# Attention followed by a SoLU feed-forward: the order of POOL's sums and one ACT scaling at the start of the last stage, and the PSUM tiles of the first transpositions

## The chip, the cores and the metric

The kernel runs on one core of a Trainium2 chip. It has five instruction streams that run beside each other and meet at semaphores: PE (matrix multiplication and transposition, results in PSUM), ACT (activation functions and copies), DVE (elementwise work, reductions, 32x32 transposition), POOL (elementwise work on SBUF), and SP, which here issues the DMAs. The metric is the device time of one execution in microseconds, the median of several runs. Inputs and outputs are float32.

## The reference

```python
def rmsnorm(x, g):
    rms = np.sqrt(np.mean(x * x, axis=-1, keepdims=True) + 1e-06)
    return x / rms * g
q_n, k_n = rmsnorm(q, g_q), rmsnorm(k, g_k)              # 8 x 12 heads x 448 x 64
scores = (1 / np.sqrt(64)) * q_n @ k_n.transpose(0, 1, 3, 2)
attn = softmax(scores)
x = (attn @ v)  ->  (8 * 448) x (12 * 64) = 3584 x 768
h = x @ w_in                                             # 3584 x 1024
solu = h * softmax(h)
ln = (solu - mean) / np.sqrt(var + 1e-06) * g_ln
out = ln @ w_out                                         # 3584 x 768
```

## The kernel before

`fast_path` has three stages, one after the other. A slower general path stands behind a test at the end and is not taken with these inputs.

**Attention.** The 96 heads are taken as 48 pairs of heads (n), two pairs to a step (m = 0 to 23). For most pairs the rows of q and k are loaded in a blocked layout, squared on ACT (`squares`), summed on DVE (`row_sums`), folded across partitions on POOL (`fold_sums`), turned into reciprocal roots (`rsqrt_seed` on ACT, `rsqrt_step` on DVE), multiplied on POOL (`normalise`) and transposed in 32x32 blocks on DVE (`qk_transpose`). Each pair then has scores on PE, an exponential on ACT (L809), and the products with v on PE. Sums of exponentials go by DVE (`add`, L846), POOL (`add_more`, L858) and a matmul with ones.

Pairs 0 and 1, the first step, take a shorter way: `load_rows`, `square_rows`, `sum_rows`, `normalise_rows` (L775, DVE), then `transpose_rows` on PE (L783) into a PSUM tile, four transpositions for the queries (s = 0) and four for the keys (s = 1), and `take_rows` copies the result to `qkT`: the queries by ACT (L791), the keys by ACT for pair 0 (L793) and by DVE for pair 1 (L795). The order written out by hand in step 0 is: both halves of pair 0 transposed, both copied; scores 0, 1 and 2 of pair 0; then for pair 1 transposition and copy of the queries, transposition and copy of the keys; squares of pairs 2 and 3; the sums of pair 0's exponentials; and `scores_last` (L832), which makes the last 64 rows of both pairs in one tile and so needs both pairs' `qkT`.

PSUM has eight banks of 512 float32. The pool `ps_t` deals them out as three tiles with the tag "t" and one with the tag "o", of two banks each. The tag "t" serves the scores and small products in turn, each waiting until the tile three before it has been read. The tag "o" holds the products with v (`values_last`, L863) and before them the warm-up products (L764) and the first pairs' transpositions (L780).

**First product, x @ w_in.** 14 groups g of two tiles of 128 tokens (t). The multiplication is done by a scheme with seven products of half size instead of eight. When a tile's row is complete, `done` hands out its remaining steps with due times in units: `ff_max`, `ff_exp` (ACT, L1109), `ff_mult` (DVE, L1113), `ff_moments` (statistics on DVE, L1121 to L1126, then a power and a product on POOL, L1127 and L1129), `ff_norm` (ACT, L1133: the scaling) and `ff_spread` (DVE transposition L1142 and four stores by SP, L1145). The due times of the last four tiles are written out (L1154 to L1156). A unit of this stage counts 4; a step is issued after the first unit that reaches its due time.

**Last product, ln @ w_out.** Seven blocks n of four tiles, with two levels of the seven-product scheme: seven outer products (`ORDER`: P1, P5, P6, P2, P7, P3, P4), each of seven inner products of four 128x192 matmuls (L1253). Each inner product has a slot: outer product q has its seven at 7q + (0, 4, 8, 10, 12, 16, 20). A slot counts 1 in the same clock as above, so the steps still due from the stage before are issued between the first slots; a slot that holds no product only moves the clock. Side work is told to slots by `when`, and is issued after the product of its slot and after the steps that are due:

- `load_u` (SP, L1190) loads a tile's half; `make` builds an outer operand from it: a11, a12, a22 by ACT copies (L1208 to L1212), s1, s3, s4 by DVE, s2 by DVE, or in block 0 by POOL (L1216, slots 0 and 1).
- `inner_sums` makes the four sums or differences that an operand's inner products need, all on POOL (L1231 to L1234). For block 0 the sums of a11 and s1 are made in the stage before, those of s2 (operand of P6, the third outer product) at slot 5, the next ones at slot 7q - 6 (a12 at 15, s3 at 22).
- Results are taken out of PSUM by ACT copies (L1265) for P1 and P5, and by DVE additions (L1267, L1292, L1305, L1315) for the others. The inner products p1, p6, p7 and p4 accumulate in one bank A, so each of them must wait until the one before it has been read.

Each engine works through its instructions in the order in which they were issued, so the place of a call in this program is its place in the queue.

Of the kernel before, what the change touches and what calls it, by code (L numbers as in the profile page):

```python
# [9 lines left out]
FP32 = mybir.dt.float32  # L10
# [356 lines left out]
def fast_path(  # L367
# [25 lines left out]
    B, H, S, D = q.shape  # L393
    DM, DFF = moe_w_in.shape
    P = 128
# [8 lines left out]
    NG = NT // 2  # L404
# [16 lines left out]
    ps_t = banks_in.enter_context(tc.tile_pool(name="ps_t", bufs=3, space=bass.MemoryType.PSUM))  # L421
# [346 lines left out]
    def flat(x):  # L768
        return x.rearrange("p h j d -> p (h j d)")
# [6 lines left out]

    def transpose_rows(n, s):
        d = st[n]
        if s == 0:
            d["pt"] = ps_t.tile([P, 2, 512], FP32, tag="o", name="pt", bufs=1)  # L780
        d["pt", s] = d["pt"][:, s, 0:S]
        for j in range(4):
            nc.tensor.transpose(  # L783
                d["pt", s].rearrange("p (r j) -> p j r", j=4)[:, j], flat(d["sq"][:, s])[:, j * P : (j + 1) * P], ident[0:R, 0:R]
            )
# [189 lines left out]
    def load_x(g):  # L975
        x = gs[g, "x"] = xs.tile([P, KD, 2 * P], FP32, tag="x", name="xg")
        t = 2 * g * P
        while t < 2 * (g + 1) * P:
            b, c = divmod(t, S)
            n = min(S - c, 2 * (g + 1) * P - t)  # L980
            o = t - 2 * g * P

            (nc.sync if g < 2 else nc.scalar).dma_start(x[:, :, o : o + n], xd[b].rearrange("(c p) t -> p c t", p=P)[:, :, c : c + n])
            t += n

    def sizes(g):

        x = gs[g, "x"].rearrange("p c t -> p (c t)")
        n = HD * 2 * P
        sm = gs[g, "s"] = xs.tile([P, 3, HD, P], FP32, tag="x", name="xsum")  # L990
        y = sm.rearrange("p k c t -> p (k c t)")
        if g == 0:
            y = work.tile([P, 2 * NB, 32], FP32, tag="sq", name="sq", bufs=2).rearrange("p b d -> p (b d)")
        for i in range(2):
            nc.scalar.activation(
                y[:, 0:n], x[:, i * n : (i + 1) * n], AF.Square,
                accum_out=xmax[:, 2 * g + i : 2 * g + i + 1],
            )
# [7 lines left out]
    def block_sums(g, part):  # L1006

        if part == 0:
            gs[g, "A"] = x_blocks(g)
        a11, a12, a21, a22 = gs[g, "A"]  # L1010
        sm = gs[g, "s"]
        s1, s2, s4 = [sm[:, i] for i in range(3)]
        if part == 0:
            nc.gpsimd.tensor_tensor(s1, a21, a22, OP.add)
            nc.gpsimd.tensor_tensor(s2, s1, a11, OP.subtract)
        else:
            nc.gpsimd.tensor_tensor(a21, a11, a21, OP.subtract)
            nc.gpsimd.tensor_tensor(s4, a12, s2, OP.subtract)
# [81 lines left out]
    def ff_max(t):  # L1100
        d = mt[t]
        d["nmax"] = small.tile([P, 1], FP32, tag="hmax", name="hmax")
        nc.vector.tensor_scalar(d["nmax"], d["top"], -1.0, None, OP.mult)  # L1103
# [46 lines left out]
    def in_parts():  # L1150
        def done(g, i):
            t = 2 * g + i
            ff_max(t)
            waits = {  # L1154
                (NG - 2, 1): (1, 2, 3, 5, 5), (NG - 2, 0): (1, 2, 4, 6, 7),
                (NG - 1, 1): (1, 2, 3.25, 6.75, 7.25), (NG - 1, 0): (2.25, 4.25, 6.75, 8, 8.75),  # L1156
            }.get((g, i), (1, 2, 3, 5, 7))
            for x, f in zip(waits, (ff_exp, ff_mult, ff_moments, ff_norm, ff_spread)):
                later(x, lambda f=f: f(t))

        p = [products(g, lambda i, g=g: done(g, i)) for g in range(NG)]
        parts = [p[0][1], p[0][2]]
        for g in range(NG):
            turn = [p[g][6], p[g][5], p[g][7], p[g][4], p[g][3]]
            x = len(parts)
            if g + 1 < NG:
                turn[3:] = [p[g + 1][1], p[g][4], p[g + 1][2], p[g][3]]
            parts += turn
            if g + 1 < NG:
                follow(parts, x, lambda g=g: sizes(g + 1))  # L1170
                follow(parts, x + 1, lambda g=g: block_sums(g + 1, 0))
                follow(parts, x + 2, lambda g=g: block_sums(g + 1, 1))
            if g + 2 < NG:
                follow(parts, x + 4, lambda g=g: load_x(g + 2))
        return parts

    ORDER = ("P1", "P5", "P6", "P2", "P7", "P3", "P4")
    STEP = 7
# [8 lines left out]
    def load_u(n, t, h):  # L1187
        own = last.get("u", last["first"])
        r = us[n, "raw", t, h] = own.tile([P, P * HF], FP32, tag="raw", name="ur", bufs=2 if own is last["first"] else 6)
        nc.sync.dma_start(r, ud[4 * n + t][h].rearrange("g j x -> (g j) x"))  # L1190
# [31 lines left out]
    def inner_sums(n, name):  # L1222

        own = last.get("u", last["first"])
        a = us[n, name]
        sm = us[n, name, "sums"] = own.tile(
            [P, 4, KC, 4, 32], FP32, tag="sums", name="sums", bufs=2 if own is last["first"] else 4
        )
        a11, a12, a21, a22 = [a[:, t, k * KC : (k + 1) * KC] for t in range(2) for k in range(2)]
        s1, s2, s3, s4 = [sm[:, i] for i in range(4)]  # L1230
        nc.gpsimd.tensor_tensor(s1, a21, a22, OP.add)  # L1231
        nc.gpsimd.tensor_tensor(s2, s1, a11, OP.subtract)
        nc.gpsimd.tensor_tensor(s3, a11, a21, OP.subtract)  # L1233
        nc.gpsimd.tensor_tensor(s4, a12, s2, OP.subtract)  # L1234
# [104 lines left out]
    def both(n, x, t):  # L1339

        if (n, x) not in us:
            us[n, x] = out_tile(x)
        nc.vector.tensor_tensor(us[n, x][:, t], us[n, "U2" if x == "V" else "U3"][:, t], us[n, "P5"][:, t], OP.add)
        if x == "C22" and t == 0:
            store_y(n, us[n, x], 1, 1)

    def follow(p, i, f):
        g = p[i]

        def both():  # L1350
            g()
            later(1, f)

        p[i] = both
# [7 lines left out]
    def later(units, f):  # L1362
        todo.append((now + 4 * units, f))
# [49 lines left out]
    with tc.manual_schedule():  # L1413
# [10 lines left out]
        for s in range(2):  # L1424
            normalise_rows(0, s)
            transpose_rows(0, s)
# [6 lines left out]
        for m in range(NQ):  # L1433
# [21 lines left out]
            if m == 0:  # L1455
# [6 lines left out]
                for s in range(2):  # L1462
                    transpose_rows(1, s)
                    take_rows(1, s)
# [155 lines left out]
        def when(slot, f):  # L1620
            at.setdefault(slot, []).append(f)

        def made(n, name, *slots_of):
            for t, slot in enumerate(slots_of):
                when(slot, lambda t=t: make(n, name, t))

        period = STEP * len(ORDER)
        for n in range(NS):
            base = period * n
            for i, name in enumerate(ORDER):  # L1630
                q = len(ORDER) * n + i
                for place, f in zip(PLACES, outer_product(n, name, q)):
                    assert STEP * q + place not in slots
                    slots[STEP * q + place] = f
                x = HALVES[name][0]
                if q > 1:
                    when(STEP * q - 6 if q > 2 else 5, lambda n=n, x=x: inner_sums(n, x))
            for x, t, slot in (("V", 1, 31), ("V", 0, 34), ("C22", 1, 45), ("C22", 0, 52)):
                when(base + slot, lambda n=n, x=x, t=t: both(n, x, t))
            if n == 0:  # L1640
                continue
            base -= period
            at_load = (10, 11, 15, 16, 17, 18, 21, 22) if n == 1 else (4, 5, 8, 9, 10, 11, 16, 17)
            blocks = (0, 0), (1, 0), (2, 0), (3, 0), (2, 1), (3, 1), (0, 1), (1, 1)
            for slot, (t, h) in zip(at_load, blocks):
                when(base + slot, lambda n=n, t=t, h=h: load_u(n, t, h))
            late = n == 1
            made(n, "a11", base + 12 + 6 * late, base + 15 + 6 * late)
            made(n, "s1", base + 21 + 18 * late, base + 24 + 17 * late)
            made(n, "s2", base + 28 + 15 * late, base + 38 + 7 * late)  # L1650
            made(n, "a12", base + 33, base + 36)
            made(n, "s3", base + 40 + 7 * late, base + 42 + 7 * late)
            made(n, "s4", base + 47 + 4 * late, base + 49 + 4 * late)
            made(n, "a22", base + 53 + 2 * late, base + 55 + 2 * late)
# [99 lines left out]
```

## Time and profile before

| | us |
|---|---|
| timed runs: median (lowest to highest) | 801.15 (801.07 to 801.8) |
| the profiled execution: its own time | 802.04 |
| its span, first to last instruction | 800.2 |

| stretch of the span, us | length | PE busy | DVE busy | ACT busy | POOL busy | DMA share |
|---|---|---|---|---|---|---|
| 0 to 27: first step | 27.0 | 22.76 | 17.09 | 15.80 | 9.42 | 0.89 |
| 27 to 313: attention | 286.0 | 285.30 | 243.89 | 223.13 | 207.83 | 0.79 |
| 313 to 566.5: first product | 253.5 | 253.19 | 179.22 | 135.26 | 142.35 | 0.47 |
| 566.5 to 583: start of the last stage | 16.5 | 14.59 | 15.78 | 10.16 | 10.95 | 0.77 |
| 583 to the end | 217.2 | 210.61 | 153.25 | 88.94 | 153.76 | 0.49 |

How to read the lines of the profile: a line of the timeline gives the start in us from the span's beginning, the duration, the engine, the line of the kernel, the operation, output<-input by the program's names, shapes, and how many instructions were merged; in brackets how long the engine had stood idle before and which engine's work is taken to have ended the wait. PE is the matrix multiplication, PEld its weight load, which overlaps. In the list of waits the numbers are the total, the count and the longest. Who ended a wait is inferred from semaphore events.

### The profile page before, as it was taken

How to read it: one execution, taken by the hardware profiler on the slowest of the kernel's cores; microseconds unless marked ns; L12 is line 12 of the kernel's file. 1: busy time of each engine (PE TensorE's matmuls, PEld its weight loads, DVE VectorE, ACT ScalarE, POOL GpSimd, SP SyncE). 2: the span in 40 equal slices, each digit the busy share in tenths (PEclk: the TensorE clock that was granted, in tenths of full speed). 3: DMA queues.
4: the chain of work that ended last, by engine and by line, in shares of the span. 5: the costliest groups of instructions: out<-in, count | busy, mean ns of one | idle time of the engine just before them, and what ended most of it. 6: DMA issues, size and time to landing. Idle time of an engine off the chain costs nothing.

```text
span 800.2 us, 15287 instructions
## 1 busy us (share of the span) xinstructions
PE 786.5 (98%) x5382; PEld 469.2 (59%) x5382; DVE 609.2 (76%) x1153; ACT 473.3 (59%) x783; POOL 524.3 (66%) x665
## 2 busy tenths in 40 slices
PE   8999999999999999999999999999999999999997
PEld 3344444444444444444444444444789999999996
DVE  6777989889888895487777667776896776866945
ACT  6777888878778773566766544454515455464410
POOL 2666677768877785243466466668597777877861
PEclk9999999999999999999999999999999999999999
DMA  8878798998888742455555445542757557466212
GB/s 165 162 163 166 171 187 195 197 188 170 166 162 176 147 117 71 138 132 151 151 132 143 108 106 145 140 122 52 208 149 234 166 174 255 133 212 236 100 60 84
DMA packets 266913, 122.74 MB, mean 153 GB/s; under 512 B 184012, under 2 KB 251980, under 8 KB 266828
## 3 DMA queue, kind: packets, MB, share of 16 engines
q1 hardware_dynamic: 252988, 111.78, 55.9%
q10 hardware_dynamic: 13840, 9.90, 4.5%
q8 instruction: 44, 0.72, 0.4%
q14 instruction: 41, 0.34, 0.1%
HBM read 84.94 MB, written 36.70 MB: 152 GB/s over the span
## 4 chain that ended last, share of the span: by engine, by line
PE 88%; DVE 4%; POOL 2%; SPq 1%; ACT 1%; DMA 1%; issue 1%; DVEq 0%; ACTq 0%; POOLq 0%
PE A L1253 14%; PE s L819 13%; PE o L883 12%; PE BD L1038 12%; PE A L1038 12%; PE B L1253 7%; PE sm L932 5%; PE C L1038 5%; PE C L1253 3%; PE s L832 2%; PE o L869 2%; SPq L636 1%; PE o L910 1%; DMA ur<-ud 0%; DVE ub L1142 0%
## 5 line engine op out<-in xcount | busy, mean ns | idle before, releaser
L809 ACT ACTIVATE E<-s 128x896 f32<-128x896 f32 x168 | 141.4, 933 | 12.8 <-PE s L819 11.6
L819 PE MATMUL s<-qkT 64*64 64x448 f32 x1152 | 124.0, 544 | 1.6 <-ACT qkT L793 1.2
L883 PE MATMUL o<-E,v 64*64 64x448 f32 x1056 | 107.2, 536 | 0.0
L1127 POOL TENSOR_TENSOR he<-he,mhalf 128x1 f32<-128x1 f32 x28 | 27.3, 975 | 104.2 <-DVE he L1126 99.1
L819 PEld LDWEIGHTS s<-qkT 64*64 64x64 f32 x1152 | 49.8, 163 | 58.2 <-issue 25.2
L858 POOL TENSOR_TENSOR es<-es,E 128x896 f32<-128x896 f32 x23 | 49.1, 2135 | 51.4 <-DVE es L846 51.4
L1253 PE MATMUL A<-w_out,sums 128*128 128x192 f32 x392 | 80.1, 327 | 2.2 <-POOL sums L1233 1.3
L1253 PE MATMUL B<-w_out,sums 128*128 128x192 f32 x392 | 79.9, 326 | 0.4 <-DVE P L1315 0.4
L713 POOL TENSOR_TENSOR qkn<-qk,ny 128x896 f32<-128x896 f32 x46 | 77.1, 1697 | 3.5 <-DVE ny L707 1.5
L1038 PE MATMUL A<-w_in,xg 128*128 128x512 f32 x168 | 74.6, 593 | 0.0
L883 PEld LDWEIGHTS o<-E,v 64*64 64x64 f32 x1056 | 40.6, 133 | 58.0 <-issue 58.0
L1109 ACT ACTIVATE u<-h,hmax 128x1024 f32<-128x1024 f32 x28 | 32.2, 1151 | 66.8 <-DVE hmax L1103 66.8
L1038 PE MATMUL BD<-w_in,xsum 128*128 128x512 f32 x156 | 71.2, 592 | 0.0
L1253 PEld LDWEIGHTS A<-w_out,sums 128*128 128x128 f32 x392 | 66.1, 190 | 3.3 <-POOL sums L1233 1.6
L1253 PEld LDWEIGHTS B<-w_out,sums 128*128 128x128 f32 x392 | 66.3, 190 | 0.8 <-DVE P L1315 0.7
L846 DVE TENSOR_TENSOR es<-E 128x896 f32<-128x896 f32 x48 | 56.9, 1189 | 0.7 <-ACT E L809 0.7
L1038 PEld LDWEIGHTS A<-w_in,xg 128*128 128x128 f32 x168 | 31.8, 190 | 40.1 <-issue 39.3
L723 DVE STREAM_TRANSPOSE qkT<-qkn 128x896 f32<-128x896 f32 x46 | 50.9, 1106 | 4.1 <-POOL qkn L713 4.1
L1038 PEld LDWEIGHTS BD<-w_in,xsum 128*128 128x128 f32 x156 | 29.5, 190 | 37.5 <-issue 35.2
L690 POOL COPY ss<-part 32x56 f32<-32x56 f32 x92 | 47.1, 512 | 6.1 <-DVE part L680 1.9
L680 DVE TENSOR_REDUCE part<-sq 128x28 f32<-128x896 f32 x46 | 47.8, 1077 | 2.2 <-ACT sq L672 2.2
L1253 PE MATMUL A<-w_out,s 128*128 128x192 f32 x224 | 45.7, 326 | 0.0
(160 smaller groups left out, 1665.5 us busy)
## 6 DMA issues: line engine op xcount, KB each, us to landing
ur<-ud SPq DMA_DIRECT2D x60, 256.0 KB, 4.4
ud<-ub SPq DMA_DIRECT2D x112, 128.0 KB, 2.3
xd<-xo SPq DMA_DIRECT2D x48, 224.0 KB, 3.0
qk<-in_q_dram SPq DMA_DIRECT2D x92, 112.0 KB, 3.2
qk<-in_k_dram SPq DMA_DIRECT2D x92, 112.0 KB, 3.1
v<-in_v_dram SPq DMA_DIRECT2D x24, 384.0 KB, 5.2
out_dram<-P SPq DMA_DIRECT2D x19, 384.0 KB, 3.4
raw<-in_moe_w_in_dram SPq DMA_DIRECT2D x12, 512.0 KB, 5.1
```

Of the source, the lines that this page charges most:

```text
L680: nc.vector.tensor_reduce(norms[m]["part"][:, i], st[n]["sq"], AX, OP.add)
L690: e.tensor_copy(ss[g * 32 : g * 32 + 32], part[o * 32 : o * 32 + 32])
L713: e.tensor_tensor(d["qkn"].rearrange("p (s b) d -> p s b d", s=2), d["qk"].rearrange("p s (b d) -> p s b d", d=32), y.rearrange("p (s b) - ...
L723: nc.vector.transpose(d["qkT"].rearrange("p s t -> p (s t)"), d["qkn"].rearrange("p b d -> p (b d)"))
L809: nc.scalar.activation(d["E", kc], s[:, :, 0:S], AF.Exp)
L819: nc.tensor.matmul(s[c : c + D, h, 0:S], d["qkT"][hh, 1, keys], d["qkT"][hh, 0, :], start=True, stop=True,)
L846: nc.vector.tensor_tensor(d["es"], d["E", 0], d["E", 1], OP.add)
L858: e.tensor_tensor(d["es"], d["es"], d["E", 2], OP.add)
L883: x = nc.tensor.matmul(d["o"][h * D : (h + 1) * D, :], quads[m]["v"][pp, i + 2 * h, kc], d["E", kc][pp, h], start=False, stop=(part == 1 a ...
L932: nc.tensor.matmul(sm[g : g + 32, :], ones[:, w], e[:, h, t * S // 2 : (t + 1) * S // 2], start=(x == 0), stop=(x == len(terms) - 1),)
L1038: nc.tensor.matmul(k[bank], a[:, c], w_in[i][:, c], start=begin and c == 0, stop=c == HD - 1, skip_group_check=not begin,)
L1253: nc.tensor.matmul(k[bank], a[:, c].rearrange("p a i -> p (a i)"), w_out[:, area, i, c], start=begin and c == 0, stop=c == KC - 1, skip_gr ...
```

## The change

Three edits. In `transpose_rows` every group of four transpositions gets a PSUM tile of its own and uses the first of its two banks: the tag is "o" for pair 1's queries, and "t" for pair 0's queries and keys and for pair 1's keys. In the due times of tile 0 of group NG - 2 (the last but one group) the scaling `ff_norm` is due at 6.25 units instead of 6, one slot later: it is issued after the first product of the last stage and no longer ahead of it. The sums of s2 for block 0 are told to slot 2 instead of slot 5; POOL's part of `ff_moments` of the tile that is due between them (group NG - 1, tile 1, due at 3.25 units, issued after slot 4) comes behind them and no longer ahead.

```diff
     def transpose_rows(n, s):
         d = st[n]
-        if s == 0:
-            d["pt"] = ps_t.tile([P, 2, 512], FP32, tag="o", name="pt", bufs=1)
-        d["pt", s] = d["pt"][:, s, 0:S]
+        pt = ps_t.tile([P, 2, 512], FP32, tag="o" if n and s == 0 else "t", name="pt", bufs=1 if n and s == 0 else 3)
+        d["pt", s] = pt[:, 0, 0:S]
         for j in range(4):
             nc.tensor.transpose(
...
-                (NG - 2, 1): (1, 2, 3, 5, 5), (NG - 2, 0): (1, 2, 4, 6, 7),
+                (NG - 2, 1): (1, 2, 3, 5, 5), (NG - 2, 0): (1, 2, 4, 6.25, 7),
                 (NG - 1, 1): (1, 2, 3.25, 6.75, 7.25), (NG - 1, 0): (2.25, 4.25, 6.75, 8, 8.75),
...
                 if q > 1:
-                    when(STEP * q - 6 if q > 2 else 5, lambda n=n, x=x: inner_sums(n, x))
+                    when(STEP * q - 6 if q > 2 else 2, lambda n=n, x=x: inner_sums(n, x))
```

## The prediction

> **What bounds the kernel now.** I read the totals first, then what TensorE itself waited for, then the order of instructions at the two places that the diff touches.
>
> ```profile
> span 800.2 us, 15287 instructions
> PE 786.5 (98%) x5382; PEld 469.2 (59%) x5382; DVE 609.2 (76%) x1153; ACT 473.3 (59%) x783; POOL 524.3 (66%) x665
> ```
>
> TensorE is busy for 98% of the span, and the chain that ends last lies on it for 88%. No edit here changes a matmul, so only TensorE's idle time can be won: 800.2 - 786.5 = 13.7 us. The stretches say where it is: 27.0 - 22.8 = 4.2 us before 27 us, 16.5 - 14.6 = 1.9 us between 566.5 and 583 us, 6.6 us after that. The list of what PE waited for has most of it at the edited lines:
>
> ```profile
> PE A L1253 <- POOL sums L1233: 1.3, 1, 1.3
> PE s L819 <- ACT qkT L793: 1.2, 1, 1.2
> PE pt L783 <- ACT qkT L791: 1.1, 1, 1.1
> PE s L832 <- ACT E L809: 0.7, 1, 0.7
> PE A L1253 <- DVE u L1267: 0.6, 2, 0.4
> PE A L1253 <- ACT q L1265: 0.6, 1, 0.6
> ```
>
> The start, in order of time:
>
> ```profile
> 8.38 1.18 PE L783 MATMUL pt<-ident,xsq 112*128 112x112 f32 x8 [0.15 <-DVE xsq L775]
> 9.66 0.64 ACT L791 ACTIVATE qkT<-pt,gcol 128x448 f32<-128x448 f32 x1 [0.17 <-PE pt L783]
> ...
> 14.26 0.65 ACT L791 ACTIVATE qkT<-pt,gcol 128x448 f32<-128x448 f32 x1
> 14.96 0.60 PE L783 MATMUL pt<-ident,xsq 112*128 112x112 f32 x4 [1.14 <-ACT qkT L791]
> 15.67 0.62 DVE L795 COPY qkT<-pt 128x448 f32<-128x448 f32 x1 [2.00 <-PE pt L783]
> 17.37 2.54 ACT L809 ACTIVATE E<-s 128x896 f32<-128x896 f32 x3 [1.16 <-PE s L832]
> ```
>
> PE writes the key half of pair 1's tile only at 14.96, 0.05 us after ACT has read the query half (14.26 + 0.65 = 14.91), though these are different halves: the one tile ties them. At 9.66 ACT reads pair 0's query half only after both halves are written (9.56).
>
> The last stage's first products:
>
> ```profile
> 567.64 1.23 ACT L1133 ACTIVATE u<-u,shift,he 128x1024 f32<-128x1024 f32 x1
> 568.77 0.30 ACT L1265 COPY q<-A 128x192 f32<-128x192 f32 x1
> 569.22 0.89 PE L1253 MATMUL A<-w_out,sums 128*128 128x192 f32 x4 [0.57 <-ACT q L1265]
> 575.09 1.49 DVE L1113 TENSOR_TENSOR u<-h,u 128x1024 f32<-128x1024 f32 x1
> 575.58 1.59 POOL L1232 TENSOR_TENSOR sums<-sums,s 128x256 f32<-128x256 f32 x1
> 577.28 0.62 ACT L1208 COPY a<-ur 128x512 f32<-128x512 f32 x1 [1.19 <-DMA ur<-ud]
> 578.17 0.92 PE L1253 MATMUL A<-w_out,s 128*128 128x192 f32 x4
> 579.85 1.18 DVE L1220 TENSOR_TENSOR s<-a,s 128x512 f32<-128x512 f32 x1
> 580.44 1.17 POOL L1233 TENSOR_TENSOR sums<-a 128x256 f32<-128x256 f32 x1
> 581.22 0.34 DVE L1267 TENSOR_TENSOR u<-A,P 128x192 f32<-128x192 f32 x1
> 581.71 0.89 PE L1253 MATMUL A<-w_out,sums 128*128 128x192 f32 x4 [1.31 <-POOL sums L1233]
> ```
>
> Groups of four matmuls start 0.65 us apart when nothing is late. The start at 569.22 is 0.73 late, 577.22 0.13, 578.17 0.30, 581.71 1.48; with what follows each, 2.9 us. The label at 581.71 names POOL, but that product (slot 26, P6's p7) reads sums finished at 578.31, and it adds to bank A, which DVE's `u<-A,P` of slot 22 must have read: that ends at 581.56. DVE is late there, having been busy almost without a break since 567.77.
>
> **The tiles of the first pairs.** Nothing is added or removed on any engine and no DMA moves; waits go. (a) Pair 0: ACT is done with its squares at 8.34 + 1.15 = 9.49 and the query half's transpositions at about 8.97, so the copy starts at 9.45 instead of 9.66. Both copies, the first scores (10.77) and all that follows come 0.2 earlier. (b) Pair 1: the key half follows the query half directly. Four transpositions take 0.60, so the second four run from 13.6 to 14.1 instead of 14.96 to 15.56, and DVE's copy starts at 14.2 instead of 15.67 (it started 0.11 behind its PE end) and ends at 14.85. ACT's copy of the query half ends at 14.7. The second half of the last-rows scores needs both copies: 14.9 instead of 16.36, so 1.45 earlier. The exponential of these (17.37) then may start at 15.9; ACT before it has squares until 15.62 + 0.60 - 0.2 = 16.0. DVE's first sum of exponentials (16.21) and the row sums move with DVE's copy; their inputs on ACT are squares ending at 15.5 and 16.0, in time for 15.7 and 16.7. POOL's sum (17.44), its fold (19.61), the reciprocal roots (21.82), the normalising (23.27) and the scores at 26.98 hang on these one behind the other. So 1.45 us arrives at 27 us.
>
> What could take it back: the new buffers. Pair 1's key half gets the buffer of the first scores, whose exponential ends at 12.77, 0.8 us before; the last-rows scores get that of the second scores, free at 13.6 for a start at 14.1. The price is whatever that margin is exceeded by. If DVE's copy still went behind ACT's (both write one `qkT`), it would start at 14.77: 0.9 instead of 1.45. Loads don't move: pair 4's squares (23.15, then 21.7) need k loads issued until 18.03, which land 3.1 us later, at 21.1; with the worst landing of the start, 4.2, at 22.2, taking 0.5. From 27 us to 313 PE is busy 285.3 of 286.0 us, so a shift passes through undiminished. Term: -1.45, between -0.9 and -1.6.
>
> **The scaling one slot later** (6 to 6.25). ACT runs `q<-A` (0.30) ahead of the scaling (1.23), not behind. PE's A is ready at 567.35, so the copy ends at 567.95 and the start at 569.22 can be 568.49. The scaling ends 0.2 to 0.3 later, near 569.1; DVE's transposition of that tile starts at 570.27 only, behind its multiply, so neither it nor SP's four stores move, and the next exponential (568.97) follows as before. The 0.7 us doesn't last: the next accumulation into A needs ACT's `u` copy (570.32 to 570.64), which leaves 0.48, and at 578.17 PE needs an `u` copy that ACT holds behind `a<-ur`, whose load was issued at 574.29, behind DVE's `s3` (573.35). Nothing there moves. Term 0, at best -0.1.
>
> **The sums ahead of the moments** (slot 5 to 2). POOL's four sums of s2 took 574.77 to 578.99. Now they follow its two subtractions, which end at 569.00. Alone a sum takes 0.73 and the next starts 0.70 later. DVE's multiply L1113 (567.77, 2.31 long, 1.22 elsewhere) is held up by the second subtraction until 569.0; then DVE or POOL goes on. The nearest row is the one at 575.09: DVE waited there for POOL's sum to end at 575.50, went next, and POOL's following sum became 1.59 long, 0.86 more than alone. So DVE goes first, and the sums run from 570.0 to 572.9, beside DVE's `P<-C,q`, transposition and statistics, which take 0.34, 1.25 and 1.28 beside POOL's sums elsewhere as they do alone. If POOL went first, DVE would be one sum late: +0.73, and with it `s3`, the load, ACT's copy and PE.
> The moments' power on POOL waits for DVE until 573.44 anyway, 0.5 us after the sums end; beyond that margin every us late goes through the scaling at 574.85 to ACT's copies and PE.
> Next on POOL are the a12 sums (578.95 to 582.3 before). Their input is ready at 571.7, so they take the s2 sums' old place, 574.77 to 579.0, with the same collisions. Then POOL is idle at 579.85, where DVE's L1220 was 1.18 beside POOL's 1.17. Alone the same line takes 0.68 (600.55) and the next starts 0.61 later, against 1.10: DVE's `u<-A,P` ends 0.49 earlier, and PE starts at 581.2 instead of 581.71. PE by itself would be ready at 580.2, so the sums at 577.22 and slot 26 no longer bind, DVE does. Everything behind hangs on PE and DVE; the later stops at 599.28 and 603.69 come from a DVE queue that starts at 591.08 on a PE result, so they shift along. Term: -0.5; from +0.2 (0.73 lost, 0.5 won) to -0.9 (PE never later than its own 580.2 plus latency).
>
> The Trainium skill bears on this in "SBUF — State Buffer", section "Who interferes with whom". It says that issue order decides who blocks, and that a VectorE instruction with two SBUF inputs and a GpSimd one that reads SBUF exclude each other for a whole instruction. It speaks against putting POOL work beside L1113: read at its strictest the last stage would lose 0.2 rather than win 0.5. The row at 575.09 has DVE going next, so I keep the row.
>
> **Sum.** -1.45 - 0 - 0.5 = about -1.95. The profiled execution took 802.04 us (span 800.2 and 1.8 around it), 0.9 above the median of the timed runs, 801.15. The terms are differences in the span, so I take them from both: 800.1 for such an execution, 799.2 for the median.
>
> **Rivals.**
> - One term is small. The head gives only 0.9 because the copies stay in order: 801.15 - 0.9 - 0.5 = 799.75. For it: they write one tile; against: the halves of `xsq` are written by DVE (4.12, 0.69) and ACT (4.49) at the same time. 12 in 100.
> - The last stage gives nothing or loses 0.2: 799.7 to 799.9. For it: POOL's first moved sum meets L1113; against: the row at 575.09. 13 in 100.
> - The head's gain is covered: the loads set the start. DMA engines are busy 89% before 27 us. Only the last stage's 0.5 is left: 800.65. Against: the usual landing is 0.6 us ahead of need. 8 in 100.
> - Slower: in the last stage each of the four moved sums gets in ahead of a DVE instruction of the queue that sets 578.17 and 581.71. DVE is 4 x 0.73 = 2.9 late, the a12 sums are pushed back too so the 0.5 isn't won: 801.15 - 1.45 + 2.9 = 802.6. It decides from 1.45 us of lateness on. Against: from 570 to 573 us no large DVE instruction reads two operands from SBUF, and such ones show no lengthening beside POOL. 5 in 100.
> - The forecast, 799.2, its own range 798.6 to 799.6: 62 in 100.
>
> **How the numbers follow.** Range: the forecast's low end, 798.5 (-1.6, -0.9 and a little), up to the covered head, 800.8; outside are the slower case and some unforeseen, under 2 in 10. About 0.2% (1.6 us) is what a measurement here tells from no change, so 799.55 parts faster from same. Faster: nearly all of the forecast's 62 and a few of the near ones, 0.64. Slower by 0.2% needs more than the slower rival's 802.6: 0.05. Same: 0.31.
>
> **What would show it.** Right: no wait of PE at L783 on ACT; the last-rows scores' second half near 14.9; scores of pair 2 at about 25.5 instead of 26.98; `q<-A` before the scaling; POOL's s2 sums ending near 573; L1220's second instruction near 0.68; slot 26 about 0.5 sooner after 566.5 than now (15.2 us). Wrong: PE at 26.98 unmoved (loads), L1113 over 2.31 (POOL first), the power on POOL behind the sums, or PE stops in slots that had none.

## The result, and the profile after

| | before, us | after, us |
|---|---|---|
| timed runs side by side: median (lowest to highest) | 801.77 (801.07 to 802.30), 12 runs | 799.78 (799.10 to 801.65), 12 runs |
| ratio after / before, 95% interval | | 0.9978 (0.9970 to 0.9985) |
| the profiled execution: its own time, span | 802.04, 800.2 | 799.27, 797.5 |

The kernel became 1.99 us faster by the medians. The two profiled spans differ by 2.7 us. Single executions of one kernel scatter by 1 us and more, so the traces tell where time went, and the medians how much. The runs of before fall into two groups, near 801.2 and near 802.1, so its median depends on how many of each a comparison caught (801.31 to 801.81 in those below). In the changed kernel every line from L782 on has a number one lower than before (L783 is L782, L1253 is L1252).

The totals of the page of after:

```profile
span 797.5 us, 15285 instructions
PE 786.1 (99%) x5382; PEld 468.7 (59%) x5382; DVE 608.1 (76%) x1153; ACT 472.2 (59%) x783; POOL 524.3 (66%) x665
```

Busy times are as before (PE 786.5, POOL 524.3): work has not become less, TensorE's idle time has, from 13.7 to 11.4 us. What PE waited for (total, count, longest, in us):

```profile
PE A L1252 <- DVE u L1266: 1.4, 3, 0.8
PE pt L766 <- DVE warm L763: 1.4, 1, 1.4
PE s L818 <- ACT qkT L792: 0.8, 1, 0.8
PE s L831 <- ACT E L808: 0.7, 1, 0.7
PE B L1252 <- DVE P L1314: 0.4, 1, 0.4
PE s L818 <- ACT qkT L727: 0.4, 1, 0.4
PE BD L1037 <- DVE top L1053: 0.2, 1, 0.2
PE pt L782 <- DVE xsq L775: 0.2, 1, 0.2
```

Three lines of before have gone: the transpositions' wait for ACT (1.1), the wait put down to POOL's sums (1.3) and the one for `q` (0.6). The wait for the first `qkT` is 0.8 instead of 1.2, and DVE's `u` is named where POOL was.

The start of after, in order of time:

```profile
8.26 1.27 PE L782 MATMUL pt<-ident,xsq 112*128 112x112 f32 x8 [0.18 <-DVE xsq L775]
9.24 0.61 ACT L790 ACTIVATE qkT<-pt,gcol 128x448 f32<-128x448 f32 x1
...
12.77 0.99 PE L782 MATMUL pt<-ident,xsq 112*128 112x112 f32 x8
...
13.80 0.62 DVE L794 COPY qkT<-pt 128x448 f32<-128x448 f32 x1 [0.58 <-PE pt L782]
13.81 0.65 ACT L790 ACTIVATE qkT<-pt,gcol 128x448 f32<-128x448 f32 x1
...
15.64 2.55 ACT L808 ACTIVATE E<-s 128x896 f32<-128x896 f32 x3
...
25.24 2.22 PE L818 MATMUL s<-qkT 64*64 64x448 f32 x20 [0.39 <-ACT qkT L727]
```

The eight transpositions of pair 1 now run in one go of 0.99 us, where before two groups of four began 1.7 us apart. ACT and DVE read their halves at the same time (13.81, 13.80). The scores of pair 2 begin at 25.24 instead of 26.98. Counted from the first transposition (8.38 before, 8.26 after, a difference that belongs to the start of the execution) it is 18.60 against 16.98: 1.62 us. From there nothing changes until the last stage: between the first score of pair 2 and the first product of the last stage lie 539.5 to 539.6 us in before, in after and in every kernel below.

The first products of the last stage, the first of them in before and then the rows of after:

```profile
566.54 0.81 PE L1253 MATMUL A<-w_out,a 128*128 128x192 f32 x4
...
564.77 0.81 PE L1252 MATMUL A<-w_out,a 128*128 128x192 f32 x4
...
565.73 0.30 ACT L1264 COPY q<-A 128x192 f32<-128x192 f32 x1
565.86 2.31 DVE L1112 TENSOR_TENSOR u<-h,u 128x1024 f32<-128x1024 f32 x1
565.93 1.24 ACT L1132 ACTIVATE u<-u,shift,he 128x1024 f32<-128x1024 f32 x1
...
567.17 1.59 POOL L1230 TENSOR_TENSOR sums<-s 128x256 f32<-128x256 f32 x1
...
575.22 0.62 ACT L1207 COPY a<-ur 128x512 f32<-128x512 f32 x1 [1.04 <-DMA ur<-ud]
...
576.11 0.92 PE L1252 MATMUL A<-w_out,s 128*128 128x192 f32 x4
...
577.78 0.65 DVE L1219 TENSOR_TENSOR s<-a,s 128x512 f32<-128x512 f32 x1
...
578.62 0.35 DVE L1266 TENSOR_TENSOR u<-A,P 128x192 f32<-128x192 f32 x1
...
579.12 0.89 PE L1252 MATMUL A<-w_out,sums 128*128 128x192 f32 x4 [0.78 <-DVE u L1266]
```

`q<-A` is ahead of the scaling. POOL's first moved sum met DVE's multiply: DVE's took 2.31 as before, POOL's 1.59. The second L1219 takes 0.65 instead of 1.18. Slot 26 begins at 579.12, 14.35 us after the stage's first product (564.77); before it was 581.71 - 566.54 = 15.17 us.

In what follows "slot 26" stands for that distance, and "head" for the distance from the first transposition to the scores of pair 2. Before's head of 18.60 is a steady number: the other profiles with the old tiles and the old order have 18.54 to 18.58.

### The profile page after: what moved, and what is told of

Its sections match the earlier page's. It is cut to its first block, busy times and chain, and to the rows that moved or that the text cites. A ratio compares the mean times of both kernels' runs of the same rounds, so it can differ in the third digit from the quotient of the medians.

```text
span 797.5 us, 15285 instructions
## 1 busy us (share of the span) xinstructions
PE 786.1 (99%) x5382; PEld 468.7 (59%) x5382; DVE 608.1 (76%) x1153; ACT 472.2 (59%) x783; POOL 524.3 (66%) x665
## 4 chain that ended last, share of the span: by engine, by line
PE 87%; DVE 5%; SPq 2%; ACT 2%; DMA 2%; issue 1%; POOL 0%; DVEq 0%; ACTq 0%; POOLq 0%
PE A L1252 14%; PE s L818 13%; PE o L882 12%; PE BD L1037 11%; PE A L1037 11%; PE B L1252 7%; PE sm L931 5%; PE C L1037 5%; PE C L1252 3%; PE s L831 2%; PE o L868 2%; SPq L636 1%; DVE ub L1141 1%; PE o L909 1%; DMA ur<-ud 1%
## 5 line engine op out<-in xcount | busy, mean ns | idle before, releaser
L1252 PE MATMUL A<-w_out,sums 128*128 128x192 f32 x392 | 80.0, 327 | 1.3 <-DVE u L1266 1.2
L1252 PE MATMUL B<-w_out,sums 128*128 128x192 f32 x392 | 79.9, 326 | 0.4 <-DVE P L1314 0.4
L1252 PEld LDWEIGHTS A<-w_out,sums 128*128 128x128 f32 x392 | 66.2, 190 | 2.4 <-issue 1.5
L1252 PEld LDWEIGHTS B<-w_out,sums 128*128 128x128 f32 x392 | 66.3, 190 | 0.8 <-DVE P L1314 0.7
L1252 PE MATMUL A<-w_out,s 128*128 128x192 f32 x224 | 45.7, 326 | 0.1
```

What stands on the lines that cost most here:

```text
L1252: nc.tensor.matmul(k[bank], a[:, c].rearrange("p a i -> p (a i)"), w_out[:, area, i, c], start=begin and c == 0, stop=c == KC - 1, skip_gr ...
```

## The experiments

**The tiles alone.**

```diff
-        if s == 0:
-            d["pt"] = ps_t.tile([P, 2, 512], FP32, tag="o", name="pt", bufs=1)
-        d["pt", s] = d["pt"][:, s, 0:S]
+        pt = ps_t.tile([P, 2, 512], FP32, tag="o" if n and s == 0 else "t", name="pt", bufs=1 if n and s == 0 else 3)
+        d["pt", s] = pt[:, 0, 0:S]
```

> The kernel before with the tiles of the first transpositions alone; the last stage as before. My theory: the shared tile makes PE wait for ACT's copy and ACT for the second half, so PE no longer waits at the transpositions, pair 2's first scores start near 25.2 us instead of 26.98, and about 1.6 us arrives at the end: time 0.9980 of before. The stretch from the last stage's first product to slot 26 (P6's p7) stays at 15.0 to 15.2 us. Rival (loads set the start): pair 2's scores stay near 26.9 and the time is that of before. Rival (the head's gain is used up in the attention stage): scores at 25.2, but the last stage's first product still at 566.5.

Measured: 799.50 us against 801.31, ratio 0.9971 (0.9960 to 0.9982); head 16.81, slot 26 15.02. So this edit alone gives, within the intervals, what the whole change gives.

**The scaling alone.**

```diff
-                (NG - 2, 1): (1, 2, 3, 5, 5), (NG - 2, 0): (1, 2, 4, 6, 7),
+                (NG - 2, 1): (1, 2, 3, 5, 5), (NG - 2, 0): (1, 2, 4, 6.25, 7),
```

> The kernel before with the one scaling a slot later alone. My theory: the stop of 0.73 us at slot 8 goes, but PE still stops at slots 23 and 26, which hang on a load behind ACT and on DVE, so from the last stage's first product to slot 26 it is 15.0 to 15.2 us as before; the time is within 0.1% of before. Rival (the gain at slot 8 lasts): slot 26 at 14.5 and the time 0.5 to 0.7 us lower.

Measured: 801.59 against 801.31, ratio 0.9997 (0.9988 to 1.0006). PE's stop of 0.73 us in slot 8 is gone, and slot 26 is at 15.17, exactly where it was: the time comes back as longer stops in slots 12, 22 and 23.

**The sums alone.**

```diff
-                    when(STEP * q - 6 if q > 2 else 5, lambda n=n, x=x: inner_sums(n, x))
+                    when(STEP * q - 6 if q > 2 else 2, lambda n=n, x=x: inner_sums(n, x))
```

> The kernel before with POOL's s2 sums at slot 2 alone. My theory: the stop at slot 8 stays (0.7), POOL's a12 sums take the old place of the s2 sums, DVE's second L1220 falls from 1.18 to 0.66 and slot 26 comes 0.5 us sooner after the last stage's first product, 14.6 instead of 15.17; time 0.9994 of before. Rival (the sums need the scaling's move to win anything): slot 26 stays at 15.0 to 15.2. Rival (POOL's moved sums hold up DVE): L1113 over 2.31 us, slot 26 later than 15.2.

Measured: 801.67 against 801.31, ratio 1.0003 (0.9994 to 1.0012); slot 26 at 15.06, a gain of 0.11 us where about 0.5 was expected. By that number alone this is the rival that the sums need the scaling's move to win anything. Its timeline shows another cause:

```profile
577.71 0.62 ACT L1208 COPY a<-ur 128x512 f32<-128x512 f32 x1 [1.61 <-DMA ur<-ud]
...
578.58 0.36 DVE L1305 TENSOR_TENSOR P<-B,u 128x192 f32<-128x192 f32 x1 [0.58 <-ACT u L1265]
...
580.27 0.65 DVE L1220 TENSOR_TENSOR s<-a,s 128x512 f32<-128x512 f32 x1
```

The forecast 0.65 is there. But ACT's copy `a<-ur` waited 1.61 us for its load (1.19 before), ACT's `u` copy stands behind it, and so DVE stood still for 0.58 us (0.17 before) ahead of `P<-B,u`. From the load's issue to the copy it was 3.62 us here, 2.99 in before.

**The order alone.** The kernel before, with one line added in step 0: both groups of pair 1's transpositions are called before the two copies, still into one tile.

```diff
                 for s in range(2):
                     transpose_rows(1, s)
+                for s in range(2):
                     take_rows(1, s)
```

> The kernel before, one shared tile, with the order alone changed: both halves of pair 1 are transposed before either is copied. It tells what the sharing costs beyond the order. If only PE's write waits for ACT's read, the key half's transpositions run at 13.6 and DVE copies at 14.2, as with separate tiles, and pair 2's scores start near 25.4. If the two reads of a shared tile are kept in order as well, DVE's copy starts only when ACT's has ended, near 14.95, the last rows' second half near 15.7, and pair 2's scores start near 26.1, so half of the gain is the order's and half the tile's.

Measured: one run of 800.98; head 17.77, scores of pair 2 at 26.32. The timeline of it at pair 1:

```profile
13.31 0.99 PE L783 MATMUL pt<-ident,xsq 112*128 112x112 f32 x8
...
14.36 0.65 ACT L791 ACTIVATE qkT<-pt,gcol 128x448 f32<-128x448 f32 x1
...
15.03 0.62 DVE L795 COPY qkT<-pt 128x448 f32<-128x448 f32 x1 [1.27 <-ACT qkT L791]
15.71 0.59 PE L832 MATMUL s<-qkT 64*64 64x448 f32 x2 [0.52 <-DVE qkT L795]
```

The transpositions run in one go here too, but DVE's copy waits for ACT's to end (14.36 + 0.65 = 15.01): with one tile, its two readers on different engines go one after the other. The head is 0.83 us shorter than before's: about the 0.9 instead of 1.45 which the prediction kept as a bound. In the changed kernel both still write one `qkT` and go together, so the shared PSUM tile tied them, not `qkT`.

**Pair 1's keys alone in a tile of their own.** Pair 0 keeps one tile.

```diff
+        pt = ps_t.tile([P, 2, 512], FP32, tag="t", name="pt", bufs=3) if n and s else d["pt"]
-        d["pt", s] = d["pt"][:, s, 0:S]
+        d["pt", s] = pt[:, s, 0:S]
```

> The kernel before with one edit: only the keys of pair 1 get a PSUM tile of their own; pair 0 keeps one tile for both halves. My working puts 0.2 us on pair 0's copy and the rest on pair 1: pair 0's ACT copy stays at about 9.66, the eight transpositions of pair 1 run in one go of about 0.99 from about 13.2, and the scores of pair 2 start at 25.3 to 25.5 (before 26.98, with the whole change 25.24). Rival (pair 0's part gives nothing, ACT's copy only moves a wait): 25.1 to 25.25, as with the whole change. Rival (the gain is made by order and jitter): 26.3, as where only the order was changed.

Measured: one run of 800.18; head 17.31. Its lines are one higher than before's:

```profile
9.49 0.63 ACT L792 ACTIVATE qkT<-pt,gcol 128x448 f32<-128x448 f32 x1 [0.72 <-PE pt L784]
...
13.05 0.98 PE L784 MATMUL pt<-ident,xsq 112*128 112x112 f32 x8
...
14.07 0.62 DVE L796 COPY qkT<-pt 128x448 f32<-128x448 f32 x1 [0.58 <-PE pt L784]
14.09 0.65 ACT L792 ACTIVATE qkT<-pt,gcol 128x448 f32<-128x448 f32 x1
```

So pair 1 gives 18.60 - 17.31 = 1.29. Scores at 25.53 are 0.03 above the range that was expected, and 0.19 counted from the same start (the first transposition is at 8.22 here, 8.38 before).

One profile against one would leave pair 0's part of 1.62 - 1.29 = 0.33 uncertain, but the head can be split at the first scores in every profile. From these to the scores of pair 2 it is 16.20 to 16.21 us with the old tiles and order, 14.93 here, and 14.92 to 14.96 in seven of the eight profiles with the whole edit: pair 1's part is 1.25 to 1.29. In the eighth, the second profile of the changed kernel, it is 15.21: ACT's squares (L672, at 21.52) had waited there for a load.

From the first transposition to the first scores it is 2.32 to 2.39 us with one tile for pair 0 and 1.89 to 2.32 with two. Pair 0's part is therefore 0 to 0.5, and in five of the eight 0.4 to 0.5.

**The sums of a12 late.** The kernel before, with the next four sums on POOL pushed out of the way of DVE.

```diff
-                    when(STEP * q - 6 if q > 2 else 5, lambda n=n, x=x: inner_sums(n, x))
+                    when(STEP * q - 6 if q > 3 else (5, 22)[q - 2], lambda n=n, x=x: inner_sums(n, x))
```

> The kernel before with one edit: the four a12 sums on POOL are told to slot 22 instead of 15, so that they stand behind the last tile's power and product on POOL and not beside DVE's L1113 (the fourth), L1220 and the copies. My theory (slot 26 waits for DVE's u<-A,P, and DVE is slowed by POOL's sums beside it, the wait's label POOL is not the cause): DVE's second L1220 is about 0.65 alone instead of 1.18, its first 0.68, the last multiply 1.23, and slot 26 starts 14.2 to 14.7 us after the first product instead of 15.17; the sums then come too late for a later product, which is 2 us or more late. Rival (slot 26 does read a POOL sum, as the label of the wait said): slot 26 waits for the moved sums, about 20 us after the first product.

Measured: one run of 804.0.

```profile
579.51 0.64 DVE L1220 TENSOR_TENSOR s<-a,s 128x512 f32<-128x512 f32 x1
...
580.35 0.34 DVE L1267 TENSOR_TENSOR u<-A,P 128x192 f32<-128x192 f32 x1
...
580.83 0.89 PE L1253 MATMUL A<-w_out,sums 128*128 128x192 f32 x4 [0.78 <-DVE u L1267]
...
585.18 0.92 PE L1253 MATMUL A<-w_out,sums 128*128 128x192 f32 x4 [2.16 <-POOL sums L1232]
```

Slot 26 begins 14.38 us after the first product though the sums named in before's wait run only after 583 us: the label POOL at 581.71 in before was not the cause, DVE's `u<-A,P` was. How much of the 0.8 us is owed to the moved sums this run doesn't tell: the load came earlier in it (2.67 us from issue to copy), and DVE had no pause ahead of `P<-B,u`. The 0.8 us are lost again at the product that does need the sums, 2.3 us late.

**The load taken out of ACT's way.** The changed kernel, with ACT's two a11 copies of block 1 made at slots 25 and 27.

```diff
-            made(n, "a11", base + 12 + 6 * late, base + 15 + 6 * late)
+            made(n, "a11", base + 12 + 13 * late, base + 15 + 12 * late)
```

> The changed kernel with one edit more: ACT's two a11 copies of block 1 (they wait for a load that landed 2.9 to 3.6 us after its issue) are made at slots 25 and 27 instead of 18 and 21, behind ACT's u and P copies. Theory A (DVE's own queue, busy without a break, sets slot 26, and the load only slot 23): slot 23 (0.29 late after the change) isn't late any more, DVE's addition P<-B,u follows without its 0.09 pause, slot 26 starts 14.1 to 14.3 us after the first product instead of 14.34, the time is 799.4 to 799.8 beside 799.78. Theory B (the load's landing sets slot 26 through ACT's copy): slot 26 comes 0.5 or more sooner, at 13.8 or less, and the time is about 799.2.

Measured: 799.41 against 801.81, ratio 0.9971 (0.9961 to 0.9982). Slot 23 has no stop, slot 26 is at 14.23: theory A by the trace.

**That, and the transposition of the last group's tile 1 later** (due at 7.75 units instead of 7.25).

> The kernel with the later a11 copies of block 1 and, beside that, the transposition and stores of tile 1 of the last group due at 7.75 units instead of 7.25, behind DVE's q<-A,P and u<-A,P. If DVE's queue sets slot 26 (theory A): slot 26 is not or hardly late, at 12.7 to 13.3 us after the first product instead of 14.34; part of it is lost again a few slots later, since the queue on DVE holds the same work; the time falls by 0.2 to 0.8 us, to about 799.2. If the load sets it (theory B): slot 26 at 13.8 or later, time as with the later copies alone.

Measured: 799.61 against 801.81, ratio 0.9975 (0.9965 to 0.9985). Slot 26 is at 13.53, later than expected, because DVE's L1219 moved forward into POOL's sums and took 1.10 again. The next stop takes back more than was won:

```profile
578.25 0.89 PE L1252 MATMUL A<-w_out,sums 128*128 128x192 f32 x4
...
581.71 0.92 PE L1252 MATMUL A<-w_out,s 128*128 128x192 f32 x4 [0.62 <-DVE u L1266]
```

From the first to the last product of the stage it is 227.31 us, against 226.85 with the later copies alone. DVE has the same work either way; this order of it only moved the stop, and made the stage 0.46 us longer.

**Tiles alone, whole change, and later copies on one chip.** The same three kernels side by side.

> The edit of the tiles alone, beside the whole change on one chip. If the profiled spans tell the share of the sums (227.66 - 226.97 = 0.69 us less from the first to the last product of the last stage), the whole change is 0.3 to 0.8 us faster than this kernel in the timed medians too; if the load's landing (2.9 to 3.6 us after its issue) decides as much as the sums, the two medians lie within 0.3 us. The first run of it gave a ratio of 0.9971 to before.

> The whole change again, beside the tiles alone. Sums worth what the profiles show: about 0.9965 to 0.9970 of before, 0.3 to 0.8 us under the tiles alone. Sums hidden by the load's spread: within 0.3 us of the tiles alone. The first comparison gave 0.9978, with runs from 799.1 to 801.65.

> The whole change with block 1's two a11 copies on ACT at slots 25 and 27, on the same chip. If ACT's wait for the load (2.9 to 3.6 us from issue to landing) costs the changed kernel time in part of its executions, this kernel's runs lie closer together and its median 0.2 to 0.5 us under the whole change. If DVE's queue decides alone, within 0.2 us of it.

| | median (lowest to highest), us | ratio to before (801.36) |
|---|---|---|
| tiles alone | 800.14 (799.67 to 800.99) | 0.9983 (0.9974 to 0.9992) |
| whole change | 799.80 (799.34 to 800.26) | 0.9979 (0.9970 to 0.9988) |
| whole change, copies later | 799.23 (799.19 to 799.50) | 0.9969 (0.9958 to 0.9979) |

The scaling and the sums bring 0.34 us over the tiles here; the first comparisons, on different chips, had the tiles alone in front (0.9971 to 0.9978). The intervals overlap both times. The later copies bring another 0.57 us, and their runs lie within 0.31 us of each other, those of the whole change within 0.92. In their profile PE stopped for 0.92 us at slot 16, behind another load, and slot 26 still came at 14.25: DVE's queue sets it. The profiled execution of the tiles alone was the slowest of its eleven (800.99), and in it the load landed late:

```profile
576.53 0.62 ACT L1207 COPY a<-ur 128x512 f32<-128x512 f32 x1 [1.94 <-DMA ur<-ud]
...
577.40 0.36 DVE L1304 TENSOR_TENSOR P<-B,u 128x192 f32<-128x192 f32 x1 [0.92 <-ACT u L1264]
...
579.10 1.12 DVE L1219 TENSOR_TENSOR s<-a,s 128x512 f32<-128x512 f32 x1
```

Slot 26 is at 15.72 there, 0.70 later than in the first profile of the same kernel. The second profile of the whole change has 14.42. In slot 26 the profiles put 0.6 to 1.4 us on the scaling and the sums, and the medians 0.34.

**The later copies without the scaling and the sums.** The tiles and the a11 copies, nothing else.

> The tiles, and block 1's two a11 copies at slots 25 and 27, without the scaling's and the sums' edits: against the whole change with the same later copies (ratio 0.9971 and 0.9969 to before, slot 26 at 14.23 and 14.25 us after the first product) it tells what the scaling and the sums are worth when ACT doesn't wait for the load. If the sums' move is worth the 0.5 us that I forecast for DVE's second L1220 (1.18 beside POOL, 0.65 alone): slot 26 at 14.6 to 14.9, and a ratio of about 0.9976 (0.4 to 0.6 us slower than with them). If the move was only a way past the load: slot 26 at 14.2 to 14.4 and a ratio of about 0.997.

Measured: 799.14 against 801.38, ratio 0.9972 (0.9962 to 0.9982). Slot 26 is at 14.23, the same as with the scaling and the sums, and the stage is 226.86 us long against 226.85.

```profile
576.91 0.73 POOL L1230 TENSOR_TENSOR sums<-a 128x256 f32<-128x256 f32 x1
577.56 0.64 DVE L1219 TENSOR_TENSOR s<-a,s 128x512 f32<-128x512 f32 x1
577.72 1.07 POOL L1231 TENSOR_TENSOR sums<-sums,a 128x256 f32<-128x256 f32 x1
...
578.88 0.89 PE L1252 MATMUL A<-w_out,sums 128*128 128x192 f32 x4 [0.78 <-POOL sums L1231]
```

POOL's a12 sums are in their old place, and still L1219 takes 0.64. DVE starts it 0.16 us ahead of POOL's second sum, and POOL's becomes the long one (1.07). The rows of before:

```profile
578.15 0.36 DVE L1305 TENSOR_TENSOR P<-B,u 128x192 f32<-128x192 f32 x1 [0.17 <-ACT u L1265]
...
579.76 0.72 POOL L1232 TENSOR_TENSOR sums<-sums,a 128x256 f32<-128x256 f32 x1
```

There DVE started L1220 at 579.85, 0.09 us behind POOL's second sum, and took 1.18. Relative to POOL, DVE came 0.25 us too late, the size of its pause for ACT's `u` copy: `P<-B,u` starts 0.51 us behind the addition ahead of it in before, and 0.27 here.

The other profiles with the sums in their old place show what that costs. DVE's pause is what `P<-B,u` starts later than those 0.27 us (the idle time in brackets is 0.07 less), and the lag is counted from the start of the POOL sum that is under way when L1220 begins:

| profile | DVE's pause | lag behind POOL's sum | duration | lag + duration | slot 26 |
|---|---|---|---|---|---|
| tiles and later copies | 0 | ahead by 0.16 | 0.64 | | 14.23 |
| before | 0.24 | 0.09 | 1.18 | 1.27 | 15.17 |
| order alone | 0.36 | 0.20 | 1.07 | 1.27 | 15.01 |
| scaling alone | 0.36 | 0.21 | 1.06 | 1.27 | 15.17 |
| pair 1's keys alone | 0.51 | 0.36 | 0.92 | 1.28 | 15.03 |
| tiles alone, first profile | 0.69 | 0.55 | 0.73 | 1.28 | 15.02 |
| tiles alone, second profile | 0.99 | 0.15, of the next sum | 1.12 | 1.27 | 15.72 |

Once DVE is behind, its addition ends 1.27 or 1.28 us after the start of POOL's sum, however late it came: it waits that sum out. So slot 26 moves in steps: 14.23, then 15.0 to 15.2, then 15.72. With the sums moved and DVE's order as it was, the addition takes 0.64 or 0.65 whatever the pause, and slot 26 follows the pause itself: 14.35 at 0.09, 14.42 at 0.16, and 15.06 at 0.66 in the run of the sums alone. The second theory stands in this form: the sums' move is worth nothing where ACT does not wait for the load, about 0.7 us where the wait is short, and next to nothing again where it is as long as in the run of the sums alone.

The changed kernel with the later copies is therefore a little better than without, 0.57 us on one chip (ratios 0.9971 and 0.9969 against 0.9978 and 0.9979). The tiles with the later copies alone (0.9972) were not run beside the changed kernel, and their ratio is no better than the first one of the tiles alone (0.9971).

## Why the prediction was right, and where it was not

The forecast was 1.95 us less, 799.2 for a median of 801.15. Side by side it was 1.99 less (801.77 to 799.78), and 1.56 less on another chip. The sum is right, its division is not: the tiles give most of it, 1.81 and 1.22 us by the medians where they ran alone. That 1.95 met 1.99 so closely is luck: the tiles gave a little more than forecast in the profiles, the last stage less than forecast in the medians, and the other chip is 0.4 lower.

- **The tiles: -1.45, bounds -0.9 and -1.6.** The mechanism is as told: the one tile tied the groups of transpositions to the copies and the copies to each other. Separate tiles untied both, and every later step came earlier by the same amount. The size was a little low: 1.62 in the profile of after, 1.32 to 1.79 over the eight profiles of kernels with this edit (heads 17.28 to 16.81), past the bound of 1.6 in five of them. The sum of 1.45 contains pair 0's 0.2 (it lets ACT's copy of pair 1 end at 14.7 instead of 14.91), so it leaves 1.25 for pair 1. That part measured 1.25 to 1.29 in seven profiles. The mis-sized term is pair 0's: 0.33 in after, 0 to 0.5 over the profiles. It varies, because ACT's squares, which stand ahead of pair 0's copy, started anywhere from 7.45 to 8.52 in profiles with the tiles; I had them at 8.34 and took that for fixed. The new buffers took nothing back. In the eighth profile a load took 0.3, within the 0.5 that the prediction named.
- **The lower bound of that term.** The price "if DVE's copy still went behind ACT's" exists, in the kernel where only the order is changed: there pair 1's part is 0.76 instead of 1.28, and the prediction had 0.55 between the two. My reason for doubting it (two engines write the halves of `xsq` at the same time) spoke of the tile written, and what tied them was the tile read.
- **The scaling: 0.** Right, for the reason given: the 0.73 us at slot 8 came back before slot 26.
- **The sums: -0.5, from +0.2 to -0.9.** Each row came as told: DVE went first at L1112, the four sums ended at 572.86 in the run of the sums alone (I had said 572.9), the power did not wait behind them, and L1219 fell to 0.65. Yet the edit alone gave 0.11 in the profile and nothing in the medians; scaling and sums together gave 0.34 over the tiles on one chip, with overlapping intervals. The step that failed is the sentence "Nothing there moves" on the load behind ACT's `a<-ur`: I took the landing for fixed. In profiles in which ACT waits for it, issue to copy took 2.7 to 3.6 us, a spread of 0.9 us, more than the term. I also read L1220's 1.18 as the price of having POOL beside it; it was the price of arriving 0.09 us behind POOL. In the tiles with the later copies DVE came 0.25 us sooner and took 0.64.
- **The label at slot 26.** That it was DVE and not POOL was argued from the order of events; the late a12 sums showed it.
- **The Trainium skill.** "SBUF — State Buffer", section "Who interferes with whom", says that a DVE instruction with two SBUF inputs contends with a GpSimd one that reads SBUF, and that issue order decides who blocks. The rows agree on the contention and on order: 0.16 us ahead, 0.64; 0.09 behind, 1.18. My strictest reading, a loss of 0.2, did not come: no DVE instruction was longer for the moved sums. "PSUM — Partial Sum Buffer", section "PSUM bank collisions raise a hardware error", asks for guarding by bank and quadrant. The halves of the old tile lay in different banks, so that rule alone did not ask for the order of the two readers, which cost about 0.5 us here (0.76 instead of 1.28); the program kept the whole tile in order.

What stays open: why the later copies bring 0.57 us in the medians, when the profiled last stages of the two kernels differ by 0.1 to 0.2 us (226.97 and 227.07 against 226.85 and 226.89). Late landings in executions that were not profiled would explain it, but no run shows one in the changed kernel, and the narrower runs are no proof: the tiles with the later copies, which don't wait for the load either, range over 1.12 us (798.95 to 800.07). Nor did any run show what makes the load's landing vary.

## What to carry to other kernels

Two halves of one on-chip tile do not become independent by lying in different banks; this program kept them in order. Where two engines read them, or one writes while another reads, give each half a tile of its own and look for the wait to vanish. Before you move work to free an engine, ask what made its victim late: here the collision cost nothing when DVE came 0.25 us earlier, and a transfer ahead of a copy on a third engine decided when it came. A term smaller than the run-to-run spread of a transfer on its path can't be forecast from one trace, and shouldn't be claimed from one.

## What the runs showed of the hardware

- ACT and DVE reading the two halves of one PSUM tile went one after the other (14.36 to 15.01, then 15.03). With two tiles they read at 13.80 and 13.81, and neither was longer for it (0.62 and 0.65).
- The same DVE addition (L1220 in before) took 0.64 when it began 0.16 us ahead of a POOL sum, and POOL's sum then took 1.07 instead of 0.72. When it began 0.09 to 0.55 us behind one, in seven profiles, it ended 1.27 or 1.28 us after the start of POOL's sum.
- The load of 256 KB ahead of ACT's `a<-ur` took 2.7 to 3.6 us from issue to the copy's start in profiles in which ACT waited for it, and DVE's pause that follows from it was between 0 and 0.99 us.
- Eight 112x112 float32 transpositions in a row took 0.98 or 0.99 us, four alone 0.60.
